# Attention and a two-layer product: the second product by Strassen's seven half-size products, block sums on VectorE

## Chip, cores and metric

One core of a Trainium2 chip runs the whole program. The metric is the time of one execution on the device, in microseconds (us), lower is better. TensorE (PE in the profile) multiplies, VectorE (DVE) and ScalarE (ACT) work elementwise, GpSimd (POOL) and SyncE (SP) mostly issue DMAs here.

## The reference, cut to what matters

```
# q, k, v: 4 batches x 8 heads x 768 positions x 64
scores = q @ k.T / sqrt(64)
# heads 0, 2, 6: causal mask; heads 1, 3, 4, 5, 7: causal, and only the first 4 keys or the last 64
a = softmax(where(mask, scores, -1e9))
x = (a @ v)                      # laid out as 3072 tokens x 512
h = x @ w_in                     # 512 -> 2048
g = maximum(0.01 * h, h)
out = g @ w_out                  # 2048 -> 512, float32
```

Matrices are held in bfloat16 on the chip, sums in float32. "Product 1" below is `x @ w_in`, "product 2" is `g @ w_out`.

## The kernel before

**Tiling.** The 3072 tokens are cut into eight chunks of 384 (three tiles of 128). The list `ORDER` runs over them: chunks 0 to 3 are the halves of batches 0 and 1, chunks 4 to 7 those of batches 2 and 3, so that chunk n belongs to batch `ORDER[n][0]` and half `ORDER[n][1]`. For each chunk the kernel does attention, product 1 and product 2.

**Attention.** `Attention.slots` gives a list of small steps (slots). A slot issues the score matmuls of one group of keys (line 340, 375 or 320), the exponential on ScalarE (345, 380, 323) and, where a mask is needed, a multiplication on VectorE (348, 350, 384); two or three slots later the matmuls with V follow (309). After the last group of a head pair VectorE takes the reciprocal of the sums and scales (406, 408); the result is transposed, by TensorE for chunks 1 and 2 and by a DMA for the later ones (413), into `xts`. Streaming heads read V shifted by 64 positions from `vb`, which two DMAs on SP fill (146, 147); all heads read V from `va`. The keys come in by DMAs on POOL (114), are transposed by a DMA on SP (239) into `kd`, and copied by VectorE into `kt` (248, `spreads`), two halves of 64 partitions for each of three blocks. Chunk 0 has its own code (`First`).

**Product 1.** `in_slots(n)` gives 16 slots, one for each 128 of the 2048 columns. A slot is four matmuls of 384 columns (574) and one ScalarE instruction with the leaky ReLU that writes `g` (576). For chunk 0 a part is done tile by tile in `in_tile` (587, 590).

**Product 2.** `out_slots(n)` takes one tile of 128 tokens after the other: 16 matmuls of 512 columns (600) accumulate in one PSUM bank of the tag `py`, cut into five or six slots of two to four matmuls; VectorE copies the bank to an `o` tile (606) and SP stores it (609). The stationary operand is a 128 x 128 block of `g`, the moving one a row block of `w_out_bf`, which four DMAs on POOL fill (140, `load_out`). The last tile of chunk 7 is split by columns into 256 + 128 + 128, so that the end after the last matmul is short.

**Order.** It is written out by hand: nothing reorders instructions. Each engine takes its instructions in the order in which the Python code emits them. `merge` deals the slots of one list evenly among another, `tail` interleaves the last three attention slots with four others, `into` puts the copies of `spreads` between the later attention slots. In the loop over n from 2 to 7, product 1 of chunk n and product 2 of chunk n - 1 are merged, and with them the attention of chunk n + 1; the last nine of the merged slots (`keep`) come after the attention, while its transposing DMAs are under way. For n = 2 the `spreads` of chunk 4 come after everything else, and for n = 3 four slots of product 2 come first. Ahead of the loop, chunk 1's product 1 runs alone, then product 2 of chunk 0 begins with the `spreads` of chunk 2 after six of its slots.

**Buffers.** `g` is two rotating tiles of a chunk each (tag `g`); `va` and `vb` have a tile for each of four batches; `o` has six buffers; `ats4`, `at8`, `at_first`, `qt`, `qf` and `xs4` have buffers of their own. The eight PSUM banks are two each of `ph`, `psS`, `po`, `py`.

Of the kernel before, what the change touches and what calls it, by code (L numbers as in the profile page):

```python
# [21 lines left out]
def kernel(  # L22
# [60 lines left out]
    kt = [[bf(f"kt{i}_{hh}", 4, S) for hh in range(2)] for i in range(2)]  # L83
    va = [bf(f"va{i}", 6, H, D + 1) for i in range(B)]
    vb = [bf(f"vb{i}", 5, H, D + 1) for i in range(B)]
    vs = [bf(f"vs{i}", H, D + 1) for i in range(2)]
    ksink = [bf(f"ksink{i}", 4 * SK) for i in range(2)]
    ats = [bf(f"ats{i}", 3, 4, 64) for i in range(5)]
    ats4 = [bf(f"ats4{i}", 4, 4, 64) for i in range(2)]
    w_in_bf = bf("w_in_bf", KG, DF)  # L90
    w_out_bf = bf("w_out_bf", NG, DM)


# [3 lines left out]
    q0 = rot.tile([128, 3, H, D], BF16, name="q0", tag="qd", bufs=3)  # L97
    f0 = {nm: rot.tile([128, DM], FP32, name="o", tag="o", bufs=6).rearrange("p (h d) -> p h d", h=H) for nm in ("k", "q")}

# [42 lines left out]
    def v_shift(n, eng=None):  # L142
        eng = eng or nc.sync
        i, c = ORDER[n]
        lo, hi = (0, 2) if c == 0 else (2, 5)
        eng.dma_start(out=vb[i][0:64, lo:hi], in_=va[i][64:128, lo:hi])
        eng.dma_start(out=vb[i][64:128, lo:hi], in_=va[i][0:64, lo + 1 : hi + 1])

# [5 lines left out]
    def v_shift_pe(t, tag, eng, b=0):  # L154
        s = bank(tag, [128, 512], FP32)
        if b:
            for x, n, hs in ((0, 3, slice(3, 6)), (3, 2, slice(1, 8, 6))):
                c = slice(x * (D + 1), (x + n) * (D + 1))
                for e in range(2):
                    nc.tensor.matmul(s[:, c], lhsT=shift[:, e, :], rhs=va[b][:, t + e, hs, :],  # L160
                                     start=(x == 0 and e == 0), stop=(e == 1), skip_group_check=True)
            for x, n, hs in ((0, 3, slice(3, 6)), (3, 2, slice(1, 8, 6))):
                c = slice(x * (D + 1), (x + n) * (D + 1))
                nc.vector.tensor_copy(vb[b][:, t, hs, :], s[:, c].rearrange("p (h d) -> p h d", h=n))
            return
        w = 7 * (D + 1)
        for e in range(2):
            nc.tensor.matmul(s[:, 0:w], lhsT=shift[:, e, :], rhs=va[b][:, t + e, 1:H, :],
                             start=(e == 0), stop=(e == 1))
        dst, src = vb[b][:, t, 1:H, :], s[:, 0:w].rearrange("p (h d) -> p h d", h=7)  # L170
        if eng == "v":
# [35 lines left out]
    def turn_pair(n, p, tags, engs, nms="kq"):  # L207
        b, c = ORDER[n]
        if n not in qx:
            qx[n] = rot.tile([128, 4, CH], BF16, name="qt", tag="qt", bufs=1)  # L210
        for nm, tag, eng in zip(nms, tags, engs):
# [77 lines left out]
    class Attention:  # L289
# [74 lines left out]
        def stream(self, h):  # L364
# [22 lines left out]
            def do_av():  # L387
                a = box[0]
                for j in range(3):
                    t = 3 * c + j  # L390
                    ve = va[self.b][:, 0, h, :] if t == 0 else vb[self.b][:, t - 1, h, :]
                    self.av(p, hh, j, a[:, j, 0:2, :], ve)
                    self.av(p, hh, j, a[:, j, 2:4, :], va[self.b][:, t, h, :])
# [66 lines left out]
    class First:  # L460
        def __init__(self, j):
# [3 lines left out]
            if j == 0:  # L465
                self.at = rot.tile([128, H, 128], BF16, name="at8", tag="at8", bufs=1)
            else:
                self.blocks = [(kj, h) for kj in range(j, -1, -1) for h in RETR] + [None]
                self.at = bf(f"at_first{j}", len(self.blocks), 128)

# [54 lines left out]
        def av(self, half):  # L525
# [9 lines left out]
            for h in sorted(hs, key=lambda h: h not in RETR):  # L535
# [6 lines left out]
                else:  # L542
                    mm(x, x + 1, self.at_of[h][:, 0:2, :], vb[0][:, j - 1, h, :])
                    mm(x, x + 1, self.at_of[h][:, 2:4, :], va[0][:, j, h, :])
# [5 lines left out]
        def finish(self, half):  # L550
            po = self.po[half]
            linv = rot.tile([128, 4], FP32, name="linv4", tag="linv4", bufs=2)
            nc.vector.reciprocal(linv[:], po[:, :, D])
            xs = self.xs[half] = rot.tile([128, 4, D], BF16, name="xs4", tag="xs4", bufs=4)
            nc.vector.tensor_tensor(xs[:], po[:, :, 0:D], linv.rearrange("p (h o) -> p h o", o=1).to_broadcast([128, 4, D]),
# [8 lines left out]

    gs = {}
    py = {}

    def in_slots(n, tags=("ph",)):
        def tick(t):
            if n not in gs:  # L570
                gs[n] = rot.tile([128, NG, CH], BF16, name="g", tag="g", bufs=2)
            ph = bank(tags[t % len(tags)], [128, 512], FP32)
            for g in range(KG):
                nc.tensor.matmul(ph[:, 0:CH], lhsT=w_in_bf[:, g, 128 * t : 128 * t + 128],  # L574
                                 rhs=xts[n][:, g, :] if n else xts[0][:, :, g, :], start=(g == 0), stop=(g == KG - 1))
            nc.scalar.activation(out=gs[n][:, t, :], in_=ph[:, 0:CH], func=ACTF.Prelu, alpha=0.01)  # L576

        return [lambda t=t: tick(t) for t in range(NG)]

    def in_tile(t0, j, tag="ph", nt=4):  # L580
        if 0 not in gs:
            gs[0] = rot.tile([128, NG, CH], BF16, name="g", tag="g", bufs=2)
        ph = bank(tag, [128, 4, 128], FP32)
        for x in range(nt):
            t = t0 + x
            for g in range(KG):
                nc.tensor.matmul(ph[:, x, :], lhsT=w_in_bf[:, g, 128 * t : 128 * t + 128],
                                 rhs=xts[0][:, j, g, :], start=(x == 0 and g == 0),
                                 stop=(g == KG - 1), skip_group_check=True)
        nc.scalar.activation(out=gs[0][:, t0 : t0 + nt, 128 * j : 128 * j + 128], in_=ph[:, 0:nt],  # L590
                             func=ACTF.Prelu, alpha=0.01)

    def out_slots(n, tags=("py", "py", "py"), halves=False):
        slots = []

        def part(tt, lo, hi, tag, c0, c1):
            if lo == 0:
                py[n] = bank(tag, [128, 512], FP32)
            for ng in range(lo, hi):
                nc.tensor.matmul(py[n][:, 0 : c1 - c0], lhsT=gs[n][:, ng, 128 * tt : 128 * tt + 128],  # L600
                                 rhs=w_out_bf[:, ng, c0:c1], start=(ng == 0), stop=(ng == NG - 1))
            if hi == NG:
                o = rot.tile([128, DM], FP32, name="o", tag="o", bufs=6)
                b, c = ORDER[n]
                r0 = S * b + CH * c + 128 * tt
                nc.vector.tensor_copy(o[:, 0 : c1 - c0], py[n][:, 0 : c1 - c0])  # L606
                w = (c1 - c0) // 2 if halves and tt < 2 else c1 - c0
                for d in range(0, c1 - c0, w):
                    nc.sync.dma_start(out=out[r0 : r0 + 128, c0 + d : c0 + d + w], in_=o[:, d : d + w])

        for tt in range(3):
            if halves and tt == 2:
                slots.append(lambda: part(2, 0, NG, "py", 0, 256))
                slots.append(lambda: part(2, 0, NG, "psS", 256, 384))
                slots.append(lambda: part(2, 0, NG, "po", 384, 512))
                continue
            lo = 0
            for w in ([3, 3, 3, 3, 4], [3, 3, 3, 3, 4], [3, 3, 3, 3, 2, 2])[tt]:
                slots.append(lambda tt=tt, lo=lo, w=w: part(tt, lo, lo + w, tags[tt], 0, DM))
                lo += w  # L620
        return slots

# [5 lines left out]
    def tail(ms, a):  # L628

        return [a[0], ms[0], a[1], ms[1], a[2], ms[2], ms[3], *a[3:]]  # L630

    def merge(ms, as_):

        r, done = [], 0
        for j, m in enumerate(ms):
            want = (j + 1) * len(as_) // len(ms)
            r += as_[done:want] + [m]
            done = want
        return r + as_[done:]


    nc.vector.memset(blank[:], 0.0)
# [19 lines left out]
    load_in(1536, 2048)  # L662
    for i in range(3):
        load_out(i)
# [31 lines left out]

    qx[0] = bf("qf", 3, 4, 128)
    xts[0] = rot.tile([128, 3, 4, 128], BF16, name="xt", tag="xt", bufs=2)
# [86 lines left out]
    zero_keys(1, nc.vector, CH, S)  # L785
    for i in range(2, B):
        nc.vector.memset(va[i][:, :, :, D], 1.0)
    turn_dma(2)
    v_shift(2)
    load_qk(3)  # L790
    load_v(3)
    run(in_slots(1, ("ph", "psS")))
    turn_dma(3)
    load_qk(4)
    load_v(4)
    o0, o1 = out_slots(0), out_slots(1)
    run(o0[0:6])
    run(spreads(2))
    run(o0[6:12])
    v_shift(3)  # L800
    a2, m2 = Attention(2, xt_tag="ph").slots(lag=3), o0[12:] + o1[0:10]
    run(merge(m2[:10], a2[:-6]), tail(m2[10:], a2[-6:]))
    run(spreads(3))
    outs = o1[10:]

    for n in range(2, NCH):
# [13 lines left out]
        if n + 1 < NCH:  # L820
            a = Attention(n + 1, cross=True).slots(lag=2 if n > 2 else 3)
            a = into(a, extra) if n > 2 else a
        if n == 3:
            run(outs[:4])
            ms = outs[4:8] + merge(in_slots(n), outs[8:])
        else:
            ms = merge(in_slots(n), outs)
        keep = []
        if n == 2:
            ms, a, keep = ms[:-6], a[:-3], tail(ms[-6:-2], a[-3:]) + ms[-2:]  # L830
        elif a:
            ms, keep = ms[:-9], ms[-9:]
            if n > 4:
                keep.insert(1, a.pop())
        run(merge(ms, a), keep, extra if n == 2 else ())
        if n in (3, 4):
# [4 lines left out]
            load_v(n + 3)  # L841
        outs = out_slots(n) if n + 1 < NCH else out_slots(n, ("psS", "psS", "py"), True)
    run(outs)
# [35 lines left out]
```

The softmax here doesn't subtract the row's maximum and nothing guards it: scores larger than these inputs give would overflow.

## Time and profile before

Three executions took 232.66, 233.37 and 234.15 us; the median is 233.37 us. The profiled execution is told by its span, from the first to the last instruction.

| | |
|---|---|
| span of the profiled execution | 231.1 us |
| product 1, line 574: matmuls in `ph` | 448 x, 89.7 us busy |
| product 2, line 600: matmuls recorded (all forms) | in `py` 328, in `psS` 47, in `po` 16 |
| product 2, line 600: weight loads | 416 |
| leaky ReLU on ScalarE, line 576, into `g` from `ph` | 112 x 490 ns |
| copies of product 2, line 606, 512 columns | 691 ns each |
| out stores on SP: median from issue to landing | 3.4 us |
| w_out blocks on POOL: median from issue to landing | 13.2 us |

How to read it: "busy" joins overlapping instructions, and the mean time of a matmul is the time from its start to its end, while the next one starts long before that; the time for which a matmul holds TensorE is read from how many of them fit into a stretch without a gap. Some matmul records are missing (391 of 416 here), the weight loads are all there. TensorE's clock was granted in full in the whole span.

### The profile page before, as it was taken

What the parts mean: (1) busy time and instruction counts of PE and PEld (TensorE: products, weight loads), DVE (VectorE), ACT (ScalarE), POOL (GpSimd) and SP (SyncE); (2) the same over time, 40 slices, a digit from 0 to 9 for tenths busy, and PEclk for the clock granted to TensorE, in tenths of its full rate; (3) what the DMA queues carried; (4) which work ended last, traced back from release to release, by engine and by line L of the source; (5) the groups of instructions that cost most, each with busy time, mean ns of one, the idle gap of its engine ahead of it and who ended that gap; (6) DMA issues with size and microseconds to landing.
All of it is one profiled execution on the core that took longest, in us unless ns stands there. A gap on an engine that the chain in (4) does not pass through costs nothing.

```text
span 231.1 us, 5094 instructions
## 1 busy us (share of the span) xinstructions
PE 222.7 (96%) x2047; PEld 139.0 (60%) x2072; DVE 97.2 (42%) x282; ACT 126.8 (55%) x276; POOL 71.2 (31%) x88
## 2 busy tenths in 40 slices
PE   7899899999999999999999999999999999999995
PEld 4688766645665666566556655665556665555554
DVE  7786866033557254748124441245213341111121
ACT  5677756704756886375476436675466764333300
POOL 8997635019239029314180225300000000000000
PEclk9999999999999999999999999999999999999999
DMA  9999999999999999999299995995210220111112
GB/s 129 160 177 166 202 208 169 178 145 157 145 235 198 191 177 139 177 195 164 66 118 129 134 172 101 157 162 134 62 48 0 65 81 20 45 45 45 46 48 92
DMA packets 111977, 29.37 MB, mean 127 GB/s; under 512 B 102993, under 2 KB 108497, under 8 KB 111953
## 3 DMA queue, kind: packets, MB, share of 16 engines
q0 software_dynamic: 77552, 13.37, 78.9%
q1 hardware_dynamic: 33344, 15.41, 35.1%
q10 hardware_dynamic: 1056, 0.26, 0.5%
q8 instruction: 16, 0.26, 0.5%
q14 instruction: 9, 0.07, 0.1%
HBM read 27.30 MB, written 6.29 MB: 145 GB/s over the span
## 4 chain that ended last, share of the span: by engine, by line
PE 84%; DMA 7%; POOL 4%; DVE 2%; issue 1%; ACT 0%; POOLq 0%
PE py L600 31%; PE ph L574 30%; PE po L309 7%; PE psS L340 5%; DMA w_in_bf<-in_moe_w_in_dram 4%; PE psS L600 3%; DMA kb<-in_k_dram 3%; PE psS L375 2%; PE psS L574 2%; POOL va L119 2%; PE psS L320 2%; DVE kt L248 1%; POOL k L105 1%; POOL q L106 1%; POOL kb L114 1%
## 5 line engine op out<-in xcount | busy, mean ns | idle before, releaser
L574 PE MATMUL ph<-xt,w_in_bf 128*128 128x384 bf16 x448 | 89.7, 326 | 0.5 <-DMA w_in_bf<-in_moe_w_in_dram 0.5
L600 PE MATMUL py<-w_out_bf,g 128*128 128x512 bf16 (+1 forms) x328 | 85.5, 374 | 1.3
L576 ACT ACTIVATE g<-ph 128x384 bf16<-128x384 f32 x112 | 54.9, 490 | 54.5 <-PE ph L574 54.2
L574 PEld LDWEIGHTS <-w_in_bf 128*128 128x128 bf16 x480 | 43.8, 98 | 30.8 <-DMA w_in_bf<-in_moe_w_in_dram 0.7
L600 PEld LDWEIGHTS <-g 128*128 128x128 bf16 x416 | 36.0, 98 | 26.8
L345 ACT ACTIVATE at<-psS 128x384 bf16<-128x384 f32 x78 | 37.2, 489 | 20.2 <-PE psS L340 19.5
L606 DVE COPY o<-py 128x512 f32<-128x512 f32 (+1 forms) x22 | 14.9, 679 | 52.8 <-PE py L600 52.4
L114 POOL DMA_DIRECT2D kb<-in_k_dram x21 | 18.6, 899 | 49.0 <-DMA kd<-kb 48.0
L340 PE MATMUL psS<-qd,kt 128*128 128x384 bf16 (+2 forms) x90 | 23.3, 294 | 0.2 <-DVE kt L248 0.2
L119 POOL DMA_DIRECT2D va<-in_v_dram x24 | 21.5, 913 | 3.0 <-DMA w_out_bf<-in_moe_w_out_dram 1.8
L114 POOL DMA_DIRECT2D qb<-in_q_dram x21 | 18.6, 910 | 5.9 <-DMA w_in_bf<-in_moe_w_in_dram 2.6
L309 PE MATMUL po<-va,at 128*128 128x65 bf16 x228 | 19.2, 193 | 0.0
L380 ACT ACTIVATE ats<-psS 128x384 bf16<-128x384 f32 x35 | 16.8, 490 | 2.6 <-PE psS L375 2.3
L384 DVE TENSOR_TENSOR ats<-ats,m_win 128x384 bf16<-128x384 bf16 x35 | 12.3, 357 | 13.5 <-ACT ats L380 12.8
L309 PEld LDWEIGHTS <-at 128*128 128x128 bf16 x234 | 14.9, 98 | 5.1 <-issue 0.2
L248 DVE COPY kt<-kd 64x512 bf16<-64x512 bf16 x36 | 14.3, 396 | 3.5 <-DMA kd<-kb 3.0
L408 DVE TENSOR_TENSOR xs<-po,linv 128x384 bf16<-128x384 f32 x27 | 15.0, 557 | 0.9
L340 PEld LDWEIGHTS <-kt 128*128 128x128 bf16 x99 | 9.4, 98 | 7.5 <-DVE kt L248 0.4
L375 PEld LDWEIGHTS <-kt 128*128 128x128 bf16 x210 | 10.4, 98 | 4.5 <-issue 0.2
L350 DVE TENSOR_TENSOR at<-at,m_caus 128x128 bf16<-128x128 bf16 x21 | 4.8, 234 | 19.7 <-ACT at L345 19.6
L309 PEld LDWEIGHTS <-ats 128*128 128x128 bf16 x210 | 10.5, 97 | 4.3 <-DVE xs L408 0.4
L406 DVE RECIPROCAL linv<-po 128x6 f32<-128x6 f32 x27 | 5.2, 192 | 16.4 <-PE po L309 16.4
(144 smaller groups left out, 202.1 us busy)
## 6 DMA issues: line engine op xcount, KB each, us to landing
out_dram<-o SPq DMA_DIRECT2D x21, 256.0 KB, 3.4
va<-in_v_dram POOLq DMA_DIRECT2D x24, 128.0 KB, 8.2
kb<-in_k_dram POOLq DMA_DIRECT2D x21, 128.0 KB, 6.0
qb<-in_q_dram POOLq DMA_DIRECT2D x21, 128.0 KB, 6.8
w_out_bf<-in_moe_w_out_dram POOLq DMA_DIRECT2D x4, 512.0 KB, 13.2
vb<-va SPq DMA_DIRECT2D x8, 195.0 KB, 3.7
w_in_bf<-in_moe_w_in_dram POOLq DMA_DIRECT2D x3, 512.0 KB, 8.8
out_dram<-o SPq DMA_DIRECT2D x5, 128.0 KB, 1.8
```

The costliest lines, as they stand in the source:

```text
L114: nc.gpsimd.dma_start(out=t[:, g], in_=nat[nm][b, c, :, :, g])
L119: nc.gpsimd.dma_start(out=va[b][:, 3 * c + g, :, 0:D], in_=nat["v"][b, c, :, :, g])
L248: nc.vector.tensor_copy(kt[b % 2][hh][r, :, o : o + 128], raw["kx", n][r, g])
L309: nc.tensor.matmul(o, lhsT=lhsT, rhs=rhs, start=first, stop=False, skip_group_check=True)
L340: nc.tensor.matmul(s[:, off : off + w], lhsT=kt[i][hh][:, p, 128 * kj : 128 * kj + 128], rhs=q_of(n, p, lo, CH), start=(j == 0), stop=(j = ...
L345: nc.scalar.activation(out=a[:, 0:off], in_=s[:, 0:off], func=ACTF.Exp, scale=SM)
L375: nc.tensor.matmul(s[:, 64 * m : 64 * m + 64], lhsT=kt[i][hh][:, p, k0 : k0 + 128], rhs=q_of(n, p, 64 * m, 64 * m + 64), start=(m == 0), s ...
L380: nc.scalar.activation(out=av_, in_=s[:, 0:CH].rearrange("p (j e f) -> p j e f", j=3, e=2), func=ACTF.Exp, scale=SM)
L408: nc.vector.tensor_tensor(xs[:], po[:, :, :, 0:D], linv.to_broadcast([128, 3, 2, D]), op=ALU.mult)
L574: nc.tensor.matmul(ph[:, 0:CH], lhsT=w_in_bf[:, g, 128 * t : 128 * t + 128], rhs=xts[n][:, g, :] if n else xts[0][:, :, g, :], start=(g == ...
L576: nc.scalar.activation(out=gs[n][:, t, :], in_=ph[:, 0:CH], func=ACTF.Prelu, alpha=0.01)
L600: nc.tensor.matmul(py[n][:, 0 : c1 - c0], lhsT=gs[n][:, ng, 128 * tt : 128 * tt + 128], rhs=w_out_bf[:, ng, c0:c1], start=(ng == 0), stop= ...
```

## The change

Two tiles of 128 tokens make a pair. With A the 256 x 2048 block of `g` and B = `w_out`, cut into A11, A12 (first tile, first and second half of the 2048), A21, A22 (second tile) and B11 to B22, the four half-size results are formed from seven products instead of eight (the form of Strassen's scheme with 15 sums, after Winograd):

- block sums of A: S1 = A21 + A22, S2 = S1 - A11, S3 = A11 - A21, S4 = A12 - S2 (VectorE, 128 x 1024 bfloat16 each)
- block sums of B, once: W1 = B12 - B11, W2 = B22 - W1, T3 = B22 - B12 (in the place of B12), W4 = B21 - W2, in two halves (`weight_sums`)
- P1 = A11 B11, P2 = A12 B21, P3 = S4 B22, P4 = A22 W4, P5 = S1 W1, P6 = S2 W2, P7 = S3 T3, each of eight matmuls of 256 columns
- P2 accumulates on P1 in one bank, P7 and P4 on P6 in a second, P3 on P5 in a third; partial results are read between them: ScalarE copies P1 and the sum with P2, VectorE adds to P1's copy or to earlier results when P6, P7, P5, P4 and P3 end.

Twelve pairs cover the 24 tiles: each chunk gives one pair of two of its three tiles, and the tiles left over (`spare`) of an even and the following odd chunk make another. `steps(k)` gives the 14 half products of pair k as slots, with the block sums of pair k + 1 after P5, P4 and P3 and the fourth sum of pair k after P1. Slots now carry a cost in us (`costing`), and `merge` deals by it; `last_of` counts back the slots that make up a given time.

To make room, `va` and `vb` have three tiles and batch 3 uses those of batch 0, `vb` is without head 0, `g` is one tile of seven slabs, `o` has five buffers, and several small tiles share rotating buffers. The blocks of `w_out` are loaded in the order 0, 2, 1, 3.

```diff
-    va = [bf(f"va{i}", 6, H, D + 1) for i in range(B)]
-    vb = [bf(f"vb{i}", 5, H, D + 1) for i in range(B)]
+    va = [bf(f"va{i}", 6, H, D + 1) for i in range(3)]
+    vb = [bf(f"vb{i}", 5, H - 1, D + 1) for i in range(3)]
+    va.append(va[0])
+    vb.append(vb[0])
...
-    ats4 = [bf(f"ats4{i}", 4, 4, 64) for i in range(2)]
+    ats4 = [rot.tile([128, 4, 4, 64], BF16, name="ats4", tag="sum", bufs=6) for i in range(2)]
...
+    NH, DH = NG // 2, DM // 2
+    w1, w2, w4 = (bf(f"w_sum{i}", NH, DH) for i in (1, 2, 4))
+    g_all = bf("g_all", 7, NG, 128)
...
-            qx[n] = rot.tile([128, 4, CH], BF16, name="qt", tag="qt", bufs=1)
+            qx[n] = rot.tile([128, 4, CH], BF16, name="qt", tag="qd", bufs=3)
...
-                self.at = bf(f"at_first{j}", len(self.blocks), 128)
+                tag, bufs = ("sum", 6) if j == 1 else ("kd", 2)
+                self.at = rot.tile([128, len(self.blocks), 128], BF16, name="at_first", tag=tag, bufs=bufs)
...
-            nc.scalar.activation(out=gs[n][:, t, :], in_=ph[:, 0:CH], func=ACTF.Prelu, alpha=0.01)
+            nc.scalar.activation(out=g_all[:, slab(n) : slab(n) + 3, t, :],
+                                 in_=ph[:, 0:CH].rearrange("p (j t) -> p j t", j=3), func=ACTF.Prelu, alpha=0.01)
...
+    def weight_sums(half):
+        r = slice(NH // 2 * half, NH // 2 * half + NH // 2)
+        sub = lambda o, x, y: nc.vector.tensor_tensor(o[:, r], x[:, r], y[:, r], op=ALU.subtract)
+        sub(w1, T3, B11)
+        sub(w2, B22, w1)
+        sub(T3, B22, T3)
+        sub(w4, B21, w2)
...
+        UNITS = ("P1", "P6", "P2", "P7", "P5", "P4", "P3")
...
+        def sum(self, i):
+            assert all(done[n] == NG for n, _ in self.rows)
+            x, y, op = {1: (self.a21, self.a22, ALU.add), 2: (self.s.get(1), self.a11, ALU.subtract),
+                        3: (self.a11, self.a21, ALU.subtract), 4: (self.a12, self.s.get(2), ALU.subtract)}[i]
+            self.s[i] = rot.tile([128, NH, 128], BF16, name="sum", tag="sum", bufs=6)[:]
+            nc.vector.tensor_tensor(self.s[i], x, y, op=op)
...
+        def unit(self, u, half):
+            lo, hi = (0, NH // 2) if half == 0 else (NH // 2, NH)
+            bank_of = {"P1": "a", "P2": "a", "P6": "y", "P7": "y", "P4": "y", "P5": "x", "P3": "x"}[u]
+            first = u in ("P1", "P6", "P5")
+            lhs, rhs = {"P1": (self.a11, B11), "P2": (self.a12, B21), "P6": (self.s.get(2), w2), "P7": (self.s.get(3), T3),
+                        "P5": (self.s.get(1), w1), "P4": (self.a22, w4), "P3": (self.s.get(4), B22)}[u]
...
+                for j in range(lo, hi):
+                    nc.tensor.matmul(s[:, 0 : c1 - c0], lhsT=lhs[:, j, :], rhs=rhs[:, j, c0:c1], start=first and j == 0,
+                                     stop=(j == NH - 1), skip_group_check=True)
+                if half:
+                    self.empty(u, s[:, 0 : c1 - c0], c0, c1)
...
+        def empty(self, u, s, c0, c1):
+            add = lambda o, t: nc.vector.tensor_tensor(o, s, t[:, c0:c1], op=ALU.add)
+            if u == "P1":
+                self.o = [rot.tile([128, DM], FP32, name="o", tag="o", bufs=5) for _ in range(2)]
+                self.p1 = self.temp("p1", 2)
+                nc.scalar.activation(out=self.p1[:], in_=s, func=ACTF.Copy)
+            elif u == "P6":
+                self.u = self.temp("u", 2)
+                add(self.u[:], self.p1)
+            elif u == "P2":
+                nc.scalar.activation(out=self.o[0][:, 0:DH], in_=s, func=ACTF.Copy)
...
+            elif u == "P7":
+                self.u3 = self.temp("u3", 1)
+                add(self.u3[:], self.p1)
+            elif u == "P5":
+                add(self.o[1][:, DH + c0 : DH + c1], self.u3)
+            elif u == "P4":
+                add(self.o[1][:, 0:DH], self.p1)
+                self.store(1)
+            else:
+                add(self.o[0][:, DH + c0 : DH + c1], self.u)
...
+    def steps(k, units=Pair.UNITS, sums=True):
+        r = []
+        for u in units:
+            for half in range(2):
+                def step(u=u, half=half):
+                    pairs[k].unit(u, half)
+                    if half and u == "P1":
+                        if sums:
+                            pairs[k].sum(4)
+                    if half and 0 < k < len(pairs) - 1 and u in ("P5", "P4", "P3"):
+                        pairs[k + 1].sum({"P5": 1, "P4": 2, "P3": 3}[u])
+                r.append(costing(0.44, step))
+        return r
...
-    for i in range(3):
+    for i in (0, 2, 1):
         load_out(i)
...
-    run(in_slots(1, ("ph", "psS")))
+    weight_sums(0)
+    for i in range(1, 5):
+        pairs[0].sum(i)
+    p1 = in_slots(1, ("ph", "psS"))
+    run(p1[:14], steps(0, ("P1",), False), p1[14:])
+    weight_sums(1)
...
-    o0, o1 = out_slots(0), out_slots(1)
-    run(o0[0:6])
-    run(spreads(2))
-    run(o0[6:12])
+    run(steps(1, ("P1",), False), steps(0, ("P6", "P2", "P7")))
+    sp = spreads(2)
+    for i, u in enumerate(("P5", "P4", "P3")):
+        run(steps(0, (u,)), sp[2 * i : 2 * i + 2])
+    run(sp[6:])
+    for i in range(1, 5):
+        pairs[1].sum(i)
+    run(steps(1, ("P2",)))
     v_shift(3)
-    a2, m2 = Attention(2, xt_tag="ph").slots(lag=3), o0[12:] + o1[0:10]
-    run(merge(m2[:10], a2[:-6]), tail(m2[10:], a2[-6:]))
+    a2, m2 = Attention(2, xt_tag="ph").slots(lag=3), steps(1, ("P6", "P7", "P5", "P4", "P3")) + steps(2)
+    m2, outs = m2[:16], m2[16:]
+    at = last_of(m2, 2.6)
+    run(merge(m2[:at], a2[:-6]), tail(m2[at:], a2[-6:]))
     run(spreads(3))
-    outs = o1[10:]
...
+        ins = in_slots(n)
         if n == 3:
-            run(outs[:4])
-            ms = outs[4:8] + merge(in_slots(n), outs[8:])
+            run(outs[:8])
+            ms = merge(ins, outs[8:8]) + outs[8:]
         else:
-            ms = merge(in_slots(n), outs)
+            lead = outs[:2] + ins[:2]
+            ms = lead + merge(ins[2:], outs[2:-6]) + outs[-6:]
         keep = []
         if n == 2:
-            ms, a, keep = ms[:-6], a[:-3], tail(ms[-6:-2], a[-3:]) + ms[-2:]
+            at = last_of(ms, 3.5)
+            ms, a, keep = ms[:at], a[:-3], tail(ms[at:-2], a[-3:]) + ms[-2:]
         elif a:
-            ms, keep = ms[:-9], ms[-9:]
+            at = last_of(ms, 5.8)
+            ms, keep = ms[:at], ms[at:]
...
-        outs = out_slots(n) if n + 1 < NCH else out_slots(n, ("psS", "psS", "py"), True)
+        outs = [f for k in range(3 * n // 2, 3 * n // 2 + 1 + n % 2) for f in steps(k)]
```

## The prediction

> **What bounds the kernel now.** I read the page's engine table first, then its chain of waits, then the groups of instructions with shapes kept apart, and then single stretches of the timeline.
>
> ```profile
> span 231.1 us, 5094 instructions
> ...
> PE 222.7 (96%) x2047; PEld 139.0 (60%) x2072; DVE 97.2 (42%) x282; ACT 126.8 (55%) x276; POOL 71.2 (31%) x88
> ...
> PE 84%; DMA 7%; POOL 4%; DVE 2%; issue 1%; ACT 0%; POOLq 0%
> PE py L600 31%; PE ph L574 30%; PE po L309 7%; PE psS L340 5%; DMA w_in_bf<-in_moe_w_in_dram 4%; PE psS L600 3%; DMA kb<-in_k_dram 3%; PE psS L375 2%; PE psS L574 2%; POOL va L119 2%; PE psS L320 2%; DVE kt L248 1%; POOL k L105 1%; POOL q L106 1%; POOL kb L114 1%
> ```
>
> TensorE is the bound. The DMA and POOL shares lie ahead of 28 us. A table by stretches gives 1.44 us without TensorE work in the 163 us from 54 to 217 us, so every microsecond off TensorE counts and every new wait is paid in full. Product 2 is line 600 (31% + 3% of the chain).
>
> The groups, shapes apart, give the prices:
>
> ```profile
> L606 DVE COPY o<-py 128x512 f32<-128x512 f32 x21 | 14.5, 691 | 51.7 <-PE py L600 51.3
> L248 DVE COPY kt<-kd 64x512 bf16<-64x512 bf16 x36 | 14.3, 396 | 3.5 <-DMA kd<-kb 3.0
> L384 DVE TENSOR_TENSOR ats<-ats,m_win 128x384 bf16<-128x384 bf16 x35 | 12.3, 357 | 13.5 <-ACT ats L380 12.8
> L350 DVE TENSOR_TENSOR at<-at,m_caus 128x128 bf16<-128x128 bf16 x21 | 4.8, 234 | 19.7 <-ACT at L345 19.6
> L555 DVE TENSOR_TENSOR xs<-po,linv 128x256 bf16<-128x256 f32 x6 | 2.5, 424 | 0.2
> L590 ACT ACTIVATE g<-ph 128x256 bf16<-128x256 f32 x6 | 2.3, 390 | 0.5 <-PE ph L587 0.4
> ```
>
> The mean of a matmul (379 ns at 512 columns) is its latency, not its pitch. The pitch comes from runs without a gap, in the timeline (first line) and the chain (start, length, what):
>
> ```profile
> 45.92 8.03 PEld L600 LDWEIGHTS <-g 128*128 128x128 bf16 x38
> ...
> 224.72 1.75 PE py L600 x16
> 226.47 0.89 PE psS L600 x16
> ```
>
> The 38 matmuls of 512 columns fill 46.25 to 54.45 us: 8.20/38 = 0.216 us each. The last tile is already split: 1.75/16 = 0.1094 us for 256 columns, 0.89/16 = 0.056 for 128. Half-width matmuls thus cost half, each with its own weight load.
>
> **What the Trainium skill says.** "TensorE: Matmul & The Clock Gate", Back-to-back issue gap, gives N/2.4 + 2.5 ns: 109 and 216 ns for 256 and 512 columns; the trace agrees. The same page's specification table says that VectorE's queue is strictly first in, first out; no run here shows a counterexample, and two of my terms rest on it. "VectorE: DVE Perf Modes", the perf-mode tier table, puts a bf16 tensor_tensor in SBUF at two elements a cycle and any with a PSUM operand at one. The trace agrees: (357 - 234)/256 = 0.48 ns per element from the two masks, while line 555 (256 from PSUM) takes 424 ns.
>
> **The change, part by part.**
>
> *TensorE.* Out: 368 matmuls x 0.216 plus the split tile (1.75 + 0.89 + 0.91) = 83.0 us. In: 12 pairs x 7 products x 8 = 672, of which P5 and P3 of the last pair are cut in two: 656 x 0.1094 + 32 x 0.056 = 73.6 us. **Saved: 9.4 us**, all on the path.
>
> *VectorE.* Four sums of 1024 bf16 elements a pair: 357 + 640 x 0.48 = 0.66 us, say 0.68 with the gap. 48 of them are 32.6 us, and the eight weight sums, of the same size, 5.4. Five adds of 256 from PSUM a pair at 0.42: 25 us. Out go 24 copies, about 17 us. VectorE goes from 97 to some 143 us, 63%. Mean load is no bound; what matters is where one of these is waited for.
>
> *ScalarE.* P1 and P2 are copied there: 24 x 0.39 = 9.4 us, to 136. Where ScalarE was 80% busy (75 to 90 us: 12.03 of 15) TensorE still worked 14.89 of 15, so I take 0; at most 1 us.
>
> *New short waits on banks.* P7 must wait for the add that reads P6, P4 for that of P7, P3 for that of P5, P2 for the copy of P1. One unit (8 x 0.109 = 0.87 us) lies between. An undelayed add is over some 0.2 + 0.42 us after the last matmul, so it costs nothing unless VectorE has a queue. It has one in three places.
>
> **(a) The first pairs, about 46 to 57 us.** The second half of the weight sums waits for the last block of w_out, issued at 35.59 us and landed 10.4 later, at 46.0; it ends near 48.8. P6 needs its second half at 48.4 and has it at 47.4: no wait. After P6's add VectorE does P7's and P5's (done 52.1), then six key copies, the P4 and P3 adds between them (2.4 + 0.85, done 55.4), then the sums of pair 1, the second done at 56.8. The key copies took this long at this place:
>
> ```profile
> 50.69 2.39 DVE L248 COPY kt<-kd 64x512 bf16<-64x512 bf16 x6 [0.26 <-DMA kd<-kb]
> ```
>
> TensorE: first product done at 46.25 + 0.87 (P1 within it) = 47.1, pair 1's P1 48.0, six units to 53.2, P2 54.1, two score slots 54.4; then P6 of pair 1, which needs that second sum. **+2.3 us** (1.7 if a copy takes 0.29 as at 162 us, 2.6 above).
>
> **(b) The start of loop n = 3, about 92 us.** Eight copies (spreads of chunk 4) stand on VectorE after the tail of loop 2, and TensorE goes on with P1, P6, P2, P7 of pair 3 with nothing between. From the end T of P3: P4's add and the second sum to T + 0.7, P3's add 1.1, third sum 1.8, copies 4.9 (they took 2.83 for six here, and 0.33), fourth sum 5.6, P6's add 6.0. P7 is due at T + 2.6. At 0.29 a copy it starts at T + 4.6. **+3.0 us**, between 1.9 and 3.5. Before, output matmuls ran here under the same copies:
>
> ```profile
> 92.33 2.83 DVE L248 COPY kt<-kd 64x512 bf16<-64x512 bf16 x6
> ```
>
> **(c) The last two pairs** run without other work: between P5's end and P7, TensorE needs 5 x 0.87 = 4.37 us, VectorE 0.2 + 4 x 0.42 + 4 x 0.68 + 0.05 = 4.7. **+0.7 us** for two such joints (0 to 1.5). The tail after the last matmul stays: a 128-column add and a store.
>
> **(d) Masks held up.** In loops 2 to 6 some 55 masks now meet sums and adds ahead of them on VectorE. The trace shows one with little to spare (mask over at 164.22, its weight load at 164.27, TensorE free at 164.41). But from 92 to 117 us VectorE was 55% busy with copies of 0.69 and 0.45 us among the masks and TensorE idled 0.16 us. **+0.5 us**, 0 to 3.
>
> *Moves and buffers, taken at 0.* Blocks of w_out in order 0, 2, 1, 3: the first half of the weight sums needs blocks 0 and 2, both landed by 38 us at the latest (15.2 us after 22.6), VectorE is free at 39.5; block 1 is used at 44. No SP or POOL instruction is added for it. The fourth batch reuses the first's V: its load issues at 72.4 us, the last reader ended at 69.7; if that cover went, POOL would stand in front of the next loads, at most 1 us. The vb shifts lose head 0, so that their rows are broken into pieces; 3.7 us to landing could double, and the first reader at 59 us (itself later by (a)) is some 2 us after today's landing: 0, at most 1. Shared tags (sum, qd, kd, xs): the former users end 10 us or more before the next. Five o tiles are two and a half pairs, over 12 us, against 3.4 us for a store. Stores are 26 instead of 28. The work left between the last attention slot and the first matmul that reads its xt (5.9 us by the new costs, 6.5 before) still covers the transposing DMA (4.3 us); at (b) cover is 6.1 us instead of some 8.
>
> Sum: -9.4 + 2.3 + 3.0 + 0.7 + 0.5 = -2.9 us, span 228.2. The page gives the profiled execution's span only; the median of the three runs, 233.37, is 2.27 above it, which I carry over: **230.5 us**, 1.2% faster. About 1%, 2.3 us, is what a measurement of this kernel can tell from no change.
>
> **Rivals.** *The saving comes nearly whole* (0.28): VectorE comes to (a) and (b) without a backlog and copies at 0.29. For it: TensorE shows no slack that the change must lose. Against: the copies took 0.40 and 0.47 in just these places. With (a) 1.2, (b) 1.5 and the rest 0 to 1: 226 to 228 us. *A transfer comes late* (0.10): the key chain, load then transpose, has a period near 17.5 us (loads at 67.2, 85.0, 102.9), and a loop of 20 us is now near it; xt landing after (b) is as near. That gives 1.5 to 4 us back: 232 to 234.5. *VectorE's queue becomes the bound* (0.12, slower): masks in loops 2 to 6 wait behind sums. After (a) to (c) 3.4 us are left; at 0.06 us a mask the gain is gone, and from 0.10 us (55 x 0.10 = 5.7) the kernel is over 1% slower; one mask in four meeting a whole sum of 0.68 makes 0.17 us, 9 us, so 239 us. Against it stands the 55% stretch above. *Half-width matmuls don't cost half*: break-even is 83.0/672 = 0.1235 us; 0.1094 is measured, so this has no chance of its own.
>
> **Numbers.** My forecast (0.50) spans 229 to 232.5, some 0.36 of it more than 1% faster. Faster 0.36 + 0.28 = 0.64; same 0.14 + 0.10 = 0.24; slower 0.12. The range 226.0 to 234.3 leaves out the slower rival and the lowest 0.05.
>
> **What would show it.** Product 2 near 73.6 us at 0.109 a matmul; sums near 0.68; VectorE near 143 us. In the waits, TensorE behind a sum near 54 us for 2 us, behind P6's add near 95 us for 3 us. No such waits: first rival. Attention matmuls waiting on masks by tens: slower rival. TensorE waiting for xt or kt behind DMA: second rival. A sum at 1.1 us, or other waits above 1 us, would make it wrong.

## The result, and the profile after

| | before | changed |
|---|---|---|
| median | 233.09 us (4 runs, 232.66 to 234.15) | 230.25 us (4 runs, 230.05 to 230.39) |
| ratio | | 0.9867, 95% interval 0.9833 to 0.9900 |
| span of the profiled execution | 231.1 us | 228.3 us |

The profiled execution of the changed kernel took 230.15 us. All ratios are taken over executions within 1.5% of the fastest of their kernel, which leaves out one of the second run of both moves (233.58 us) and one of the doubled sums (252.31). The change is worth 1.3%, a third of what the seven products save. The lines of its page that answer to those shown before:

```profile
span 228.3 us, 5799 instructions
...
PE 216.3 (95%) x2344; PEld 165.8 (73%) x2344; DVE 135.2 (59%) x373; ACT 134.5 (59%) x300; POOL 71.2 (31%) x88
...
PE 76%; DVE 8%; DMA 7%; POOL 4%; issue 2%; ACT 1%; POOLq 0%; DVEq 0%; ACTq 0%
PE ph L584 30%; PE py L648 24%; DMA w_in_bf<-in_moe_w_in_dram 7%; PE po L314 6%; PE psS L345 5%; PE po L648 3%; DVE sum L631 2%; PE psS L584 2%; POOL va L124 2%; DVE kt L253 2%; PE psS L380 2%; PE psS L648 2%; PE psS L325 2%; DVE o L663 1%; DVE xs L413 1%
```

VectorE was 2% of the chain and is 8%: its sums, key copies and adds now stand in front of TensorE. Product 2 (now line 648) fell from 34% to 29%. The groups, shapes apart (out and in, count, then busy time and mean of one):

```profile
L648 PEld LDWEIGHTS <-sum 128*128 128x128 bf16 x400 | 36.8, 98 | 11.1 <-issue 2.4 <-DVE sum L631 2.3
L631 DVE TENSOR_TENSOR sum<-g_all 128x1024 bf16<-128x1024 bf16 x24 | 16.8, 700 | 0.0
L253 DVE COPY kt<-kd 64x512 bf16<-64x512 bf16 x36 | 12.0, 333 | 1.7 <-DMA kd<-kb 1.3
L663 DVE TENSOR_TENSOR o<-py,u 128x256 f32<-128x256 f32 x22 | 9.3, 421 | 10.8 <-PE py L648 10.6
```

A sum takes 0.69 us, an add 0.42, as costed. VectorE came to 135 us instead of the 143 foreseen: successive sums overlap by some 0.08 us, and busy time counts overlap once; the key copies (line 253) also came to 12.0 us instead of 14.3.

The two stalls stand where the prediction put them. TensorE's timeline (start, length, in brackets the idle time and what ended it):

```profile
53.65 1.04 PE L648 MATMUL po<-w_out_bf,g_all 128*128 128x256 bf16 x8
54.52 0.49 PE L345 MATMUL psS<-qd,kt 128*128 128x384 bf16 x2
56.94 0.61 PE L648 MATMUL py<-w_sum,sum 128*128 128x256 bf16 x4 [1.94 <-DVE sum L631]
...
94.42 1.04 PE L648 MATMUL py<-w_out_bf,g_all 128*128 128x256 bf16 x8
97.39 1.03 PE L648 MATMUL py<-w_out_bf,sum 128*128 128x256 bf16 x8 [1.93 <-DVE u L663]
```

From 53.65 to 54.52 eight matmuls of 256 columns take 0.87 us, 0.109 each. Two scores later TensorE could go on at 54.85 and starts at 56.94: 2.1 us for stall (a). P2 of pair 3 is through at 95.29 and P7 starts at 97.39: 2.1 us for stall (b). VectorE's timeline at (b):

```profile
93.34 1.09 DVE L631 TENSOR_TENSOR sum<-g_all 128x1024 bf16<-128x1024 bf16 x1
94.35 1.80 DVE L253 COPY kt<-kd 64x512 bf16<-64x512 bf16 x6
...
96.33 0.68 DVE L631 TENSOR_TENSOR sum<-g_all,sum 128x1024 bf16<-128x1024 bf16 x1
96.93 0.41 DVE L663 TENSOR_TENSOR u<-py,p 128x256 f32<-128x256 f32 x1
```

The add that P7 waits for (line 663) is the last of the block: copies, fourth sum, then it. The copies took 0.30 us each here, not 0.47.

### The profile page after: what moved, and what is told of

The parts are those of the page before. It is cut to its first block, busy times and chain, and to the rows that moved or that the text cites. A ratio compares the mean times of both kernels' runs of the same rounds, so it can differ in the third digit from the quotient of the medians.

```text
span 228.3 us, 5799 instructions
## 1 busy us (share of the span) xinstructions
PE 216.3 (95%) x2344; PEld 165.8 (73%) x2344; DVE 135.2 (59%) x373; ACT 134.5 (59%) x300; POOL 71.2 (31%) x88
## 4 chain that ended last, share of the span: by engine, by line
PE 76%; DVE 8%; DMA 7%; POOL 4%; issue 2%; ACT 1%; POOLq 0%; DVEq 0%; ACTq 0%
PE ph L584 30%; PE py L648 24%; DMA w_in_bf<-in_moe_w_in_dram 7%; PE po L314 6%; PE psS L345 5%; PE po L648 3%; DVE sum L631 2%; PE psS L584 2%; POOL va L124 2%; DVE kt L253 2%; PE psS L380 2%; PE psS L648 2%; PE psS L325 2%; DVE o L663 1%; DVE xs L413 1%
## 5 line engine op out<-in xcount | busy, mean ns | idle before, releaser
L584 PE MATMUL ph<-xt,w_in_bf 128*128 128x384 bf16 x448 | 87.8, 326 | 0.4 <-DMA w_in_bf<-in_moe_w_in_dram 0.4
L587 ACT ACTIVATE g_all<-ph 128x384 bf16<-128x384 f32 x112 | 54.9, 490 | 32.8 <-PE ph L584 31.6
L648 PEld LDWEIGHTS <-sum 128*128 128x128 bf16 x400 | 36.8, 98 | 11.1 <-issue 2.4
L648 PEld LDWEIGHTS <-g_all 128*128 128x128 bf16 x288 | 27.2, 98 | 4.1
L648 PE MATMUL py<-w_out_bf,sum 128*128 128x256 bf16 (+1 forms) x176 | 24.0, 270 | 2.1 <-DVE u L663 2.1
L648 PE MATMUL py<-w_sum,sum 128*128 128x256 bf16 (+1 forms) x176 | 23.9, 270 | 1.9 <-DVE sum L631 1.9
L663 DVE TENSOR_TENSOR u<-py,p 128x256 f32<-128x256 f32 x20 | 8.4, 421 | 22.0 <-PE py L648 18.6
L648 PE MATMUL py<-w_out_bf,g_all 128*128 128x256 bf16 x144 | 20.2, 272 | 0.0
L631 DVE TENSOR_TENSOR sum<-g_all 128x1024 bf16<-128x1024 bf16 x24 | 16.8, 700 | 0.0
L663 DVE TENSOR_TENSOR o<-py,u 128x256 f32<-128x256 f32 (+1 forms) x24 | 9.8, 410 | 10.9 <-PE py L648 10.6
```

Of the source, the lines that this page charges most:

```text
L587: nc.scalar.activation(out=g_all[:, slab(n) : slab(n) + 3, t, :], in_=ph[:, 0:CH].rearrange("p (j t) -> p j t", j=3), func=ACTF.Prelu, alp ...
L631: nc.vector.tensor_tensor(self.s[i], x, y, op=op)
L648: nc.tensor.matmul(s[:, 0 : c1 - c0], lhsT=lhs[:, j, :], rhs=rhs[:, j, c0:c1], start=first and j == 0, stop=(j == NH - 1), skip_group_chec ...
L663: add = lambda o, t: nc.vector.tensor_tensor(o, s, t[:, c0:c1], op=ALU.add)
```

## The experiments

My theory: 9.4 us are saved by half-width matmuls at half the price, and most comes back as TensorE waits for VectorE, 2.1 us each at (a) and (b), the rest in small waits. Rivals: the half-width matmuls cost more than they seem; the new buffers cost time; the stalls hide other waits. Each ratio below is to the kernel before, run on the same chip. Four chips were used, so versions that didn't run side by side are compared through these ratios and their intervals.

**The price of a half-width matmul: the kernel before with product 2 in halves.**

```diff
-                nc.tensor.matmul(py[n][:, 0 : c1 - c0], lhsT=gs[n][...], rhs=w_out_bf[:, ng, c0:c1], ...)
+                for e in range(c0, c1, 256):
+                    w = min(256, c1 - e)
+                    nc.tensor.matmul(py[n][:, e - c0 : e - c0 + w], lhsT=gs[n][...],
+                                     rhs=w_out_bf[:, ng, e : e + w], start=(ng == 0 and e == c0), ...)
```

> The kernel before, with each 512-column matmul of product 2 issued as two of 256 columns with a weight load each; same work, 368 more matmuls and weight loads. Theory (256 columns hold TensorE for 0.1094 us wherever they stand): 736 x 0.1094 - 368 x 0.2158 = +1.1 us, ratio about 1.005. Rival (the second weight load is not hidden in the stretches mixed with attention): +4 us or more, ratio above 1.015.

Measured: ratio 1.0040 (1.0024 to 1.0057), +0.9 us for 368 more weight loads. Half-width matmuls cost half also among the attention's, so the saving of 9.4 us is there, and the question is where it went.

**The buffers alone.** The kernel before with `va[3] = va[0]`, `vb` without head 0, five `o` tiles, the shared tags and the new order of `w_out` blocks:

```diff
-    va = [bf(f"va{i}", 6, H, D + 1) for i in range(B)]
+    va = [bf(f"va{i}", 6, H, D + 1) for i in range(3)]
+    va.append(va[0])
...
-    for i in range(3):
+    for i in (0, 2, 1):
         load_out(i)
```

> The kernel before with only the change's buffers: V tiles of batch 0 reused for batch 3, the shifted V without head 0, five output tiles, the shared tags, w_out blocks in the order 0, 2, 1, 3; product 2 with eight half products' worth of work as before. Theory (moves and buffers cost nothing): ratio 1.000, at most 0.002 away. Rival (the last block of w_in landing 0.5 us later, and a tail 0.3 us longer, come with the new layout): +0.4 to +1 us, ratio 1.002 to 1.004, and product 1's first full slots start near 28.3 us instead of 27.7.

Measured: ratio 1.0009 (0.9991 to 1.0027). The moves cost nothing that can be told; the interval leaves room for 0.6 us. Product 1's first full slot began at 28.6 us in this profile, the slowest of 22 executions, as the rival said. But it began at 27.5 to 28.6 in the others, and at 28.6 with the old layout too (the profile in halves), so that start is scatter, not layout.

**Stall (a) taken away: sums of pair 1 earlier.**

```diff
-    run(steps(1, ("P1",), False), steps(0, ("P6", "P2", "P7")))
+    run(steps(1, ("P1",), False), steps(0, ("P6",)))
+    for i in (1, 2):
+        pairs[1].sum(i)
+    run(steps(0, ("P2", "P7")))
...
-    for i in range(1, 5):
+    for i in (3, 4):
         pairs[1].sum(i)
```

> The first two block sums of pair 1 are issued right after P6's add of pair 0, in a stretch where VectorE waits 1.25 us for P7, instead of behind the six key copies. Theory (TensorE stands 2.1 us at 54.7 us for the second sum of pair 1): the stall goes, P6 of pair 1 follows the two score slots at once; span about 226.4 us, 2.0 below the changed kernel's 228.3 to 228.6, ratio to the kernel before about 0.978. Rival (the wait only moves to the third sum, to P6's add or to a mask behind it): under 0.8 us gained, ratio above 0.983.

Measured: ratio 0.9883 (0.9843 to 0.9923), no gain. The wait itself went: P6 of pair 1 starts at 54.64 us, right behind the two scores at 54.31. But (b) was 2.4 us long here, because its six copies took 2.51 us, and in four of six executions the mean granted clock was 0.993 (229.9 to 231.8 us); the two at full clock took 228.8 and 229.7. A cost appeared that neither theory had.

**Stall (b) taken away: key copies earlier.**

```diff
             ms, a, keep = ms[:at], a[:-3], tail(ms[at:-2], a[-3:]) + ms[-2:]
+            for j in range(4):
+                k = len(a) - 3 + 3 * j
+                a[k:k] = extra[2 * j : 2 * j + 2]
...
-        run(merge(ms, a), keep, extra if n == 2 else ())
+        run(merge(ms, a), keep)
```

> The eight key copies of chunk 4 are dealt in twos behind the last four attention slots of chunk 3 ahead of the kept work, instead of standing as a block between the third sum of pair 3 and P6's add. Theory (P7 of pair 3 stands 2.1 us at 95.3 us behind P6's add, which stands behind the copies): the stall goes; span about 226.4 us, ratio about 0.978. Rival (the bound there is the transposed attention result of chunk 3, not VectorE, or the copies now hold up masks or wait for their DMA): product 1 of chunk 3 or an attention matmul waits instead, under 0.8 us gained, ratio above 0.983.

Measured: ratio 0.9870 (0.9834 to 0.9906); the rival's number. P7 of pair 3 now follows P2 at once, but the fourth matmul of the first product slot then waits 0.63 us for the transposed attention result of chunk 3, and (a) had grown to 2.5 us.

**Both moves**, run on two chips.

> Both moves together. Theory (two independent stalls of 2.1 us each on TensorE's path): they add up, span about 224.4 us, device time about 226.2, ratio about 0.970. Rival (one of them is cover for a later transfer, so that the second gain is taken back): ratio 0.975 or above.

> Both moves alone, beside the two versions with cover on one chip: ratio about 0.981 as before, waits for the transposed queries near 55 us and for the transposed attention result near 97 us.

Measured: 228.65 us, ratio 0.9811 (0.9775 to 0.9846), and again 0.9811 (0.9765 to 0.9857). Of the 4.2 us some 1.6 were won against the changed kernel at full clock (230.2 us); on the chip where both ran side by side the medians are some 2.7 us apart (ratios 0.9811 and 0.9900), because the changed kernel often lost clock there (see "The clock"). The rival was right: (b) had been cover. TensorE's waits in the first profile (total, count, longest):

```profile
PE ph L584 <- DMA xt<-xs: 1.1, 1, 1.1
...
PE psS L345 <- DMA qd<-qb: 0.7, 1, 0.7
```

Neither line is among the waits of the changed kernel. With the stalls gone product 1 of chunk 3 comes 2.4 us earlier to its input: its fourth matmul could start at 96.7 us, and the transfer landed at 97.95. In the changed kernel it landed at 98.22, and the fourth matmul started at 99.08. The wait for the queries isn't of this kind, since the two scores that read them first stand ahead of stall (a) in both kernels. The queries landed at 54.45 us in the changed kernel, 0.07 ahead of the first score, and at 55.08 here. In the second run's profile they landed at 54.25 and nothing waited for them, against what I expected; there a matmul waited 0.7 us for the shifted V near 60 us, which is read behind (a).

**Cover for these transfers.** P6 of pair 1 is put ahead of the attention; in the first of the two kernels four attention slots of chunk 4 are also put among the eight units of pair 3.

```diff
-    run(steps(1, ("P2",)))
+    run(steps(1, ("P2", "P6")))
...
-            run(outs[:8])
+            run(merge(outs[:8], a[:4]))
+            a = a[4:]
```

> Both moves, and cover for the two transfers that then showed: P6 of pair 1 ahead of the attention of chunk 2 (0.87 us more work before its transposed queries are read, which were waited for 0.66 us), and the first four attention slots of chunk 4 dealt among the eight half products of pair 3 (about 1.2 us more before product 1 of chunk 3 reads the transposed attention result, waited for 1.1 us). Theory (the stalls behind VectorE had covered these two transfers): both waits go or fall below 0.3 us, 1.5 us less than with both moves alone, device time about 227, ratio about 0.974. Rival (another wait of the same size stands behind them, or masks of the early slots hold TensorE): ratio 0.979 or above.

> Both moves, and only P6 of pair 1 ahead of the attention of chunk 2. Theory: the wait for the transposed queries of chunk 2 goes, that of 1.1 us for the transposed attention result of chunk 3 stays; device time about 228, ratio about 0.978.

Measured: 0.9806 (0.9762 to 0.9850) with both, 0.9830 (0.9784 to 0.9876) with the first alone; neither differs from 0.9811, and both theories (0.974 and 0.978) were missed. The attention result is waited for 0.3 us where it was covered and 1.1 where it wasn't. The queries were not waited for, but they landed at 53.8 to 53.9 us in these two profiles, in time without the cover too. In the kernel with both:

```profile
PE po L314 <- DVE at L353: 1.5, 1, 1.5
PE py L648 <- DVE u L663: 1.1, 1, 1.1
```

The mask (line 353, near 107 us) stands on VectorE behind two key copies, which waited until 106.5 us for the DMA that transposes their keys. That is the key chain of the prediction's second rival. P7 of pair 1 (near 57 us) waits for P6's add, which stands behind two sums. So other waits of about the same size came in both places.

**No block sums at all.** All sums are left out, the products read blocks as they are.

```diff
-            self.s[i] = rot.tile([128, NH, 128], BF16, name="sum", tag="sum", bufs=6)[:]
-            nc.vector.tensor_tensor(self.s[i], x, y, op=op)
+            self.s[i] = {1: self.a22, 2: self.a11, 3: self.a21, 4: self.a12}[i]
```

> Leaves out all block sums, 48 of g and 8 of w_out (the seven products then read blocks as they are, and the output is another); everything else stays in its order. Theory (of the 9.4 us that seven products save, about 2.1 + 2.1 + 1.5 us are given back as waits for VectorE, and only the part caused by sums goes here): no wait at pair 1's P6; at pair 3's P7 a wait of some 0.5 us stays, since the copies remain ahead of P6's add; waits behind masks fall below 0.8 us in all; span about 224 us, ratio about 0.968. Rival (half-width products with a weight load each cost more than 0.109 us in the mixed stretches): span 226 us or more although no TensorE wait for VectorE above 0.5 us is left.

Measured: 229.02 us, ratio 0.9816 (0.9779 to 0.9853), no better than with both moves. 38 us of VectorE work gone bring some 1 us. The rival's threshold in us was met, but not by its reason: waits of 1.2 us for transposed queries (near 71 us) and 1.0 for the attention result appeared, and at (b) 1.6 us remained, three times what I expected, because the copies took longer:

```profile
92.40 3.19 DVE L252 COPY kt<-kd 64x512 bf16<-64x512 bf16 x6
```

That is 0.53 us each against 0.30 in the changed kernel. In this run POOL issued three DMAs from 91.75 to 94.46 us, under the copies; in the changed kernel its last batch ended at 92.91 and its last instruction at 93.88, before them. The Trainium skill ("SBUF — State Buffer", Who interferes with whom) says that VectorE copies in a two-port mode and POOL block each other; these two runs agree, though I varied nothing else to show it. All fourteen profiles together agree too: the 253 key copies under which no POOL instruction ran took 0.27 to 0.29 us each, and of the 251 others 119 took longer, from 0.32 to 1.05.

**Sums twice.** Each sum of g is written twice.

```diff
-            nc.vector.tensor_tensor(self.s[i], x, y, op=op)
+            for _ in range(2):
+                nc.vector.tensor_tensor(self.s[i], x, y, op=op)
```

> The changed kernel with each of the 48 block sums of g issued twice (the second writes the same values again). Theory (a sum costs TensorE only where it is waited for: two more ahead of pair 1's P6, +1.2 us; three more ahead of pair 3's P7, +1.8; the joints of the last three pairs, where VectorE then needs 0.2 + 4 x 0.42 + 8 x 0.62 = 6.8 us against 4.37, +2 us each; masks, +1.5): +8 to +9 us, ratio to the kernel before about 1.022, that is over 1% slower than it. Rival (VectorE at 59% has room and the queue settles between pairs): +4 us or less, ratio below 1.005.

Measured: 249.86 us, ratio 1.0705 (1.0679 to 1.0732), 19.6 us above the changed kernel where I expected 8 to 9. Waits of TensorE, in the profile of the execution with the lowest clock (252.31 us):

```profile
PE py L649 <- DVE sum L632: 3.8, 1, 3.8
PE py L649 <- DVE u L664: 3.1, 1, 3.1
PE po L649 <- DVE u L664: 2.8, 2, 1.4
PE po L314 <- DVE at L355: 2.7, 2, 1.6
PE py L649 <- DVE o L664: 2.3, 6, 0.6
PE po L649 <- DVE sum L632: 1.8, 2, 0.9
```

(a) and (b) grew to 3.8 and 3.1 us, and the joints (the lines with `po` and `o`) and masks that cost little before now cost several us; the clock was at 0.973 to 0.993 in all six executions, which alone is worth some 2 to 7 us (an estimate: the missing share of 250 us). VectorE's mean load is 66% of the span. So the slower rival's mechanism exists; how near to it the kernel with one sum each stands was not measured.

**The clock.** The changed kernel was run again, and once with 14 matmuls of zeros in each stall.

```diff
     run(steps(1, ("P2",)))
+    idle("psS", 14)
...
-            run(outs[:8])
+            run(outs[:6])
+            idle("psS", 14)
+            run(outs[6:8])
```

> The changed kernel itself on the same chip: ratio about 0.987, clock granted in full until the end.

> The changed kernel with 14 matmuls of 256 columns of zeros (1.53 us) put into each of the two stalls of 2.1 us, ahead of the two score slots near 54 us and between P2 and P7 of pair 3 near 95 us; their results are not read. Theory (TensorE's clock is halved for 3.4 us in some executions because TensorE stood for over 2 us, which costs 1.7 us then; work of zeros that fits into the stall takes no time): clock 0.998 or more in every execution, none above 231.2 us, median about 230.2, ratio about 0.987, the two waits shrink to some 0.5 us. Rival (the halved clock follows from the load or the chip, not from the stall): clock 0.993 in about half of the executions as without the filling. A third (the filling delays P6, P7 or the scores): median above 231.5 with full clock.

Again without filling: 13 executions, ratio 0.9900 (0.9869 to 0.9931). I had expected the full clock. Five had it and took 230.15 to 230.73 us; eight had 0.990 or 0.993 and took 230.84 to 232.89. In the profiled one of this run (b) was 2.4 us long (P7 at 97.2 us). By stretches of 2 us (TensorE busy, weight loads, VectorE, ScalarE, POOL, then the granted clock, DMA share and GB/s):

```profile
94.00:96.00 2.00, 0.92 (x9) 0.68 (x7) 1.92 (x7) 0.38 (x1) 0.27 (x1) 1.00 3.28 143
96.00:98.00 2.00, 0.82 (x5) 0.55 (x5) 1.12 (x4) 0.00 (x0) 0.00 (x0) 0.79 1.96 166
98.00:100.00 2.00, 2.00 (x10) 1.27 (x9) 0.49 (x2) 0.59 (x2) 0.00 (x0) 0.50 1.56 263
100.00:102.00 2.00, 2.00 (x24) 1.38 (x22) 0.67 (x3) 1.41 (x4) 0.00 (x0) 0.86 1.81 158
```

TensorE stands, and about when the stall ends its clock is halved: a 384-column matmul takes 0.32 us there instead of 0.163. In the profile with (a) removed the slow stretch follows (b), from 96.48 to 99.90 us, and in that with the copies early, where (b) is gone, it follows (a), from 57.39 to 60.81.

The clock's record in the traces also shows why not every execution pays. The changes lie on a grid of 3.41 us, whose start differs from execution to execution. Full clock was recorded for 92.16 us = 27 x 3.413 ahead of the first of these two stretches and for 51.2 us = 15 x 3.413 ahead of the second; each stretch lasted one step. In these two profiles and the one above, 2.4 to 2.5 us of the stall lay within one step. In the first profile of the changed kernel a step's end (at 96.65 us) cut stall (b) into 1.36 and 0.74 us, and the clock stayed full; so it did where 1.8 us lay in one step (stall (a) of the profile above). That the share of one step decides is read from these few profiles, not varied.

With the stalls filled (1.53 us of zeros each):

```profile
94.77 1.69 PE L157 MATMUL psS<-blank 128*128 128x256 bf16 x14
96.86 1.03 PE L648 MATMUL py<-w_out_bf,sum 128*128 128x256 bf16 x8 [0.40 <-DVE u L663]
```

All six executions had a clock of 0.999 or more and took 229.37 to 230.70 us, ratio 0.9886 (0.9864 to 0.9907). That fits the stall, not the load, as what halves the clock. These six alone don't prove it, since they ran on another chip and the first four executions of the changed kernel had the full clock without filling. The other runs speak for it more: on the chip of the thirteen, two of 18 executions with both moves fell to 0.991 or below, with cover or without. On another chip five of twelve executions with one stall removed fell to 0.993 or below, and none of six with both removed. Work that fits into a wait cost nothing that can be told.

## Why the prediction was right, point by point

230.5 us was forecast and 230.25 measured, span 228.2 and 228.3. The places and the mechanism were right; that the sum fits so closely is in part luck, because errors of both signs cancel:

| term | forecast | measured in the profiles |
|---|---|---|
| half-width matmuls | -9.4 us | -9.4 (0.109 each; halves alone 1.0040) |
| (a) P6 of pair 1 behind its sum | +2.3 | +2.1 |
| (b) P7 of pair 3 behind P6's add | +3.0 (1.9 to 3.5) | +2.1 |
| (c) joints of the last pairs | +0.7 | 0 |
| (d) masks; with them other small waits | +0.5 | +1.1 |
| tail, start | 0 | +0.3, +0.6 |

- *Mechanism.* Both stalls have the place, the waiting instruction and the work in front of it that were named, and taking each away removed the wait it should. The pitch formula that the prediction took from the Trainium skill ("TensorE: Matmul & The Clock Gate", Back-to-back issue gap) is given there for isolated matmuls; here it held for rows of matmuls with a weight load each.
- *(b)* was too large by 0.9 us: the term of the copies, 2.83 us for six by the row of before, measured 1.80. In the kernel before POOL was at work until 94.38 us, under these copies; in the changed kernel it was done before they began. My lower end, at 0.29 a copy, was the truth, though its sum was off: by its own terms that price gives T + 4.9, not T + 4.6, and the other price +3.4. Measured is T + 4.7.
- *(c)* was too large by all of it. Successive sums start 0.60 us apart, not 0.68, so that the four sums and four adds fit under the five products. At the first joint:

```profile
213.99 0.69 DVE L631 TENSOR_TENSOR sum<-g_all,sum 128x1024 bf16<-128x1024 bf16 x1
...
214.75 0.42 DVE L663 TENSOR_TENSOR u<-po,p 128x256 f32<-128x256 f32 x1
...
215.35 1.04 PE L648 MATMUL po<-w_out_bf,sum 128*128 128x256 bf16 x8
```

  P7 starts with the last column of P2 (at 215.35), the add having ended at 215.17.
- *(d)*: distances between successive matmul starts beyond their columns' pitch, where over 0.15 us: seven from 55 to 217 us, 1.76 us together without (a) and (b), against three and 0.7 us before. One of them, 0.33 us, is P7 of pair 1 behind P6's add. Three, 0.7 us together, are masks, as foreseen; the other three, 0.7 us, are scores that wait for ScalarE, a term that I had put at 0.
- *Tail and start.* From the end of the last matmul to the end of the span it is 3.16 to 3.18 us in every profile of the new scheme and 2.86 before; I had said that it stays. The start is scatter (buffers alone). From span to time I carried over 2.27 us; it is 1.7 to 1.9 in every execution that has both on record. The table adds up to -3.2 us; 0.4 of the measured -2.8 isn't assigned.
- *The cover of xt* was wrong, though nothing showed: I set 6.1 us of cover against 4.3, the median of all these transfers. At this place they land after 5.4 to 6.3 us in the profile of before and 6.6 to 7.3 in the changed one. Stall (b) hid it, as the kernel with both moves showed.
- *Rivals.* The first (nearly whole saving, 226 to 228 us) was not reached even without sums (median 229.02). The second (a transfer comes late) lay right behind stall (b), and with cover its key chain showed too. The slower one came true with doubled sums only.

What stays open: how much of the 9.4 us can be had. The best versions stand at 0.981. In both profiles with both moves alone, the gaps of over 0.15 us between 55 and 110 us add up to some 4.1 us, against 0.7 in the kernel before; these waits replaced each other when single ones were taken away.

## What to carry to other kernels

Fewer matmuls pay at full price only where the helper engine's results are early: for each product, add up what stands in front of its operand in that engine's queue, and compare it with the matmuls in between. Before taking a stall away, look for transfers that land under it, for they set how much of it can be won. A stall of over 2 us on TensorE can cost more than its length, so fill it with work or cut it.

## What the runs showed of the hardware

In eight of thirteen executions of the kernel with TensorE stalls of 2.0 and 2.4 us the mean clock fell to 0.990 or 0.993; in the profiled one this is a stretch at half clock that begins about where the longer stall ends. In the profile with (a) removed the clock was 0.5 for 3.4 us, which costs 1.7 us; medians with and without the loss differ by 1.7 us (231.9 and 230.2). The Trainium skill ("TensorE: Matmul & The Clock Gate", Part 1: The HAM clock gate) has the halving after an idle window of about 3.4 us, in windows that run freely. The 3.4 us of the slow stretch and the grid agree, but here a window need not be idle throughout: 2.4 us of it were enough, 1.8 were not, and none of 0.6 us (stalls filled) did it. Among 74 executions of the kernel before, whose largest gap in that part is 0.3 us, one was at 0.993 and all others at 0.998 or more.
